# A second order table for the same 2,633 steps of a softmax-attention and gated-MLP kernel, with a shorter general path

## The chip, the cores and the metric

The kernel runs on one core of one Trainium2 chip. Its time is the device time of one execution in microseconds (us), and a stated time is a median of several executions. One execution was also recorded by the hardware profiler; durations of single instructions, here and below, are from that record.

## The reference, cut to what matters

```python
def _attn_ref(q, k, v, cap):                 # (4, 12, 448, 64) each, float32
    scores = np.matmul(q, k.transpose(0, 1, 3, 2)) / np.sqrt(64)
    scores = cap * np.tanh(scores / cap)     # cap = 30
    attn = np.exp(scores - scores.max(-1, keepdims=True))
    attn = attn / (attn.sum(-1, keepdims=True) + 1e-09)
    return np.matmul(attn, v)

def _moe_ref(x, w_in, w_out):                # x: 1792 x 768, d_ff 2048
    h = x @ w_in
    g = h * (1.0 / (1.0 + np.exp(-1.702 * h)))
    return g @ w_out
```

The heads of the attention's output are put side by side to give `x` (4 batches of 448 tokens, 12 heads of 64). The weights of the second part reach the device as 64-bit numbers, and the kernel turns them into pairs of half-precision numbers itself.

## The kernel before, in words

The program has two paths. `fast_path` computes everything by sums that hold for inputs of ordinary size, and on the way it gathers evidence that they do; `verdict` (lines 1245 to 1270) turns the evidence into one integer, `flag`. `tile_kernel` (line 358) then loads `flag` into a register of every engine (line 365), and only where it is 1 does the branch at line 366 let `general_path` run, which computes the result anew in float32. With these inputs the flag is 0: each engine jumps over the code of `general_path`.

Work of the fast path. The 12 heads of a batch are taken two by two, so there are 24 pairs (units), 6 for each batch. For a pair: four groups of score products (`scores`), tanh and exp on ScalarE, row sums and products with `v` (`attend_step` and `attend`), and a division that gives two half-precision parts of `x` (`xh`, `xl`). In the first seven units scores and sums are float32 products; later ones use half-precision parts. Units 4 and 5 divide on the spot (`normalise_direct`). In the others the row sums go through memory: `sd<-f`, `rsum<-sd`, a reciprocal, `rd<-rr`, `rb<-rd`, four small transfers one after the other (lines 780 to 788), and only then is `x` formed (lines 793 to 795). An `h_unit` (line 796) adds up products of the decoded `w_in` with the `x` of pair 0, 1, ... 5 of a batch in this order; `o_unit` does so with `w_out`. Batches 2 and 3 are multiplied together with fewer products (`h_quad`, `seven_first`, `seven`). Each weight piece is fetched (`fetch_w`) and decoded (`decode_w`, lines 576 to 584) by six passes, some of which may stand on VectorE or on ScalarE.

What sets the order. Each step is entered once into a plan with the engine or engines that can do it. `schedule` unpacks the string `ORDER`: for each step its place and its engine, and for each buffer that is used in turn (a ring) the slot that each use gets. Each engine works its list strictly in order, and SyncE (SP) sends every transfer, also in order. `timed` gives each step a due time from constants (`RATE`, `LAG`, `DMA_BW`); it decides in which sequence the lists are written out, and for how long `keep_busy` (line 352) fills a planned gap of TensorE with products of zeros before the first `h_unit`. The trace of before has no such filling product.

At the start line 427 runs 16 products of `ones16` with `wz`, a tile of zeros, each 128 columns wide. At the end, after the last result (`fresh` at line 1115 and `send` at line 1072), the flag is loaded and the engines meet.

Lines as the profile names them: L257 every product of the plan, L263 every transfer, L222 most VectorE steps, L245 scaling on VectorE, L214 and L238 ScalarE, L427 the 16 products of zeros, L365 and L366 flag and branch, L1439 the end of the program.

Of the kernel before, what the change touches and what calls it, by code (L numbers as in the profile page):

```python
# [11 lines left out]
F16 = mybir.dt.float16  # L12
F32 = mybir.dt.float32
# [24 lines left out]
EV_ON = ("AV", "AV")  # L38
SPLIT_ON = "A"
# [12 lines left out]
READ_ACC = 0.083  # L52
PE_COL = 0.0004222
# [3 lines left out]
LAG = {"PE": 0.165, "ACT": 0.1, "DVE": 0.085, "SP": 2.6}  # L57
DMA_ISSUE, DMA_BW = 0.5, 0.36
# [15 lines left out]
    "wI-b@8<=EjnaQR=;GUae%9+}MbtZwSVoI2TW~xbO)|;y4wyR+_m^!9#V7tj@c9^<>BBokkr`cs%nR@1sNn~1^X=b=-6R2*kyZinbrk!bTMwoYIo@r~|n=xjj>0l0<v1X?EU>@j?W}F!nc;tGTUM8{W80c;KnDJ(}"
    "x$g#=zGgz8lNn@YnSN%u8EyKT&Vd1Dc3_41VY--=fsJO4S!m`5ewvBqp#PVdYc`pu=7=e3Hk+enfeA6cO%t=nJa%O7xV>hZd0}pvErIFgmRV)k9x$r|Vh`y>0ne^6&jLOZ#~w6(bK5L7Ndj?gQgh5~HFwPEz`np4"
    "bH%(2+%*9c&pvQh&3&`q6brmE8Et&~z<e?Z>{)ZoB)8AqLzlunHwo?aKuVj%K5@lOD*MpfFpX_4``H9dZu`Q0F?sAc^TeDt$ITK0_N99iIAOk<ljdvSlzD7kxx6-O@Pc{mirA+vG|<F;Gs-5i+7`7-1I`w+iS1k0"
    ")S@-PX7-)S6dY{A*=44=jT}s3qgZQO*w^Nw$!C)W2ia^kwSD7S+Gj4AEpF4;^7fO9YSY^AHnY8FN?5;57mQ$A*@*VD%Wosu^tN?ylr3O0*a|izINC<Dg>7^@#uf}#v_4zXR<fn+SX<d%3beIl?H5<YmJW`yZEOr1"
    "2$r**Y$4m(z6n&dU)^}y&X%#?To?P^0k*e&><1ULU2R|6&Av6Yf<tVFU~L=IX1Cp~!qc{+t!8`J33iI@X{+0zcA~9e`&o^3Y)$*!eRRX@N;}Z*u>FIp>}As{xYG`>!-K2sNNaGHooaX6x^|i!Ve8p7c2e+!U2CTY"
    "Ev~aOt;0QbvR!XC+Z@3S_J`YRx7b<sknL^v**NaHJrkT^>)Y9Oqup;W+O2khJ!@~+h4zw-?{3<h_GIvujb%gaZHsu=zObk4w%|*<$TqNd>`%AdzOqN`YrDx_wr}il`_>)^-n9?yFE_{Dvk5}y+QpV|iG641+1U1I"
    "aK61}#a#&=vz}uN=ib{#HoRMEui6j62=1}9E*#zuKC^>^5uJ0-ZEE+xMsp2=EnIkv8~WRQvIlJ%_aqo*(Is`??MM5=rgap$%$~F9+*8}yC3ERrLYKiscb{!M7s-9GKW%as*=2R?Vz{sNn~i{tY#x`<#da}6tGFnk"  # L80
    "nOt5M%jI+V-7lNXMZ^N`w-t<p1zjpv(-m^HT#C@luCS}^vb&V7jyoR&*U{w&&E@L4mZ5E2Jr^0Px=t>OYwTj+R#(mCbUR#US0ps5^RSD{?Yg=Pwu$TQVq*2sZmy^+=9H`N!dw*W?uxsnE*3U$C0yyy9<EtvNms_z"
    "aHU)#7aIq-s2B&QyJ$GjHFwc*hKq}>+)P*24RL+kEEf+4xrU+fF~s$CjofUv+-?hP>*hG0o9p~;p4;HcxqwUT%Dcpv0Qb3}F6j2VexXTlnd|9>g|4s*-Tctu?tts>D!7gApgZJrXfL<OEq9@Afm`7gyCm+gONb|2"
    "QXK4-geJn3E*Z|oBW{&j>gM5UmmDj)5pIne=|;Ju?xY*-&bqWX#!U!Khnw6)H`c9n?c6wb%58V!-OkXFxY?Z!-Hf~3D4gWd;}+cFGT>+&i)Y+9w-r<1HXMiZaSWb!$J`#A>@wno&?#;bR&p0zAuNn3u?QB$y_gwG"
    "4Nir|mBxKI9#dl`oQ#!S8f+gr4X3&}gFCqWxBw>%K99TI6fA@5LbKphoQO*>D=x+LZaU7z6?g$xVh&t}*>Dvu$FexhmBa0r7oTA<%!!Y&IOfA#SORBYZY+s;up+L-nV22RV<o(Zvv3_=!aZ&W-oU+XC$7iJxO(tS"
    "JnpLCJzRtN@fPkHTos=TzKpwZ16Ic?SO9Nh1uTdM@F3p7LwFdEU=2Jm_$qG1lXw)X;Zr<@_ptyS$7_S@;7@#xZ}0(L#}8N&PvKj9IJhn@#25Gu3)4rui|_Ff*28r43DZ-3{EENuGd942VVS5Fe!<%K8*|e)JdK&D"
# [12 lines left out]
    "|GMSBccA}Mwf{m)4gdG6|999L?ZDW-<$~1?i8a!nvgc3D?~G#g=SQiKft@w%fc}IbD6+)H5nI&oS139(^arfL*}wA1(Vyv`lk>mAe*o)%ulf"
# [49 lines left out]
class Plan:  # L148
# [158 lines left out]
    def timed(self, pre, seqs):  # L307
# [6 lines left out]
        while any(at[e] < len(s) for e, s in seqs.items()):  # L314
            moved = False
            for e, s in seqs.items():
                while at[e] < len(s) and all(start[p] is not None for p, _ in pre[s[at[e]]]):
# [9 lines left out]
                    if e == "SP":  # L327
                        done[i] = pipe = max(pipe, t + us) + o.mb / DMA_BW
# [1114 lines left out]
```

## Time and profile before

| | us |
|---|---|
| median of 3 executions (lowest, highest) | 591.7 (591.09, 592.51) |
| the profiled execution | 594.05 |
| span in it, from the first to the last instruction | 591.9 |
| TensorE busy (products) | 577.8 |
| VectorE busy | 542.0 |
| ScalarE busy | 399.3 |

Products overlap with weight loads and with each other, and their ends are modelled, so "busy" means that products were under way. The profiled execution spends 2.15 us outside its span. Engine names in rows: PE is TensorE, PEld its weight loads, DVE is VectorE, ACT is ScalarE, SP is SyncE; a q behind a name means the engine's instruction queue. The granted clock of TensorE is a column (PEclk) of the tables by stretches.

### The profile page before, as it was taken

The page shows a single profiled execution, that of the slowest core. Times are in us where ns is not written, and L with a number is a line of the kernel's source. Part 1 is how long each engine was busy: PE and PEld are TensorE (multiplying, and loading weights), DVE is VectorE, ACT ScalarE, POOL GpSimd, SP SyncE. Part 2 cuts the span into 40 slices and gives each one's busy share as a digit, 9 for nine tenths or more (in the row PEclk, how much of TensorE's full clock was granted, in tenths as well). Part 3 has the DMA queues.
Part 4 walks back from the last instruction along what each step waited for, and adds up shares of the span by engine and source line. Part 5 has one row for each costly group of instructions (what it writes and reads, how often), then busy time and mean ns, then how long its engine had stood idle before and what let it go on. Part 6 is the DMA issues. An engine that isn't in the chain of part 4 may idle for free.

```text
span 591.9 us, 9836 instructions
## 1 busy us (share of the span) xinstructions
PE 577.8 (98%) x3674; PEld 288.5 (49%) x3674; DVE 542.0 (92%) x904; ACT 399.3 (67%) x617; POOL 0.2 (0%) x4
## 2 busy tenths in 40 slices
PE   7998899999999999999999999999999999999995
PEld 3333345555555554544555555555555555555552
DVE  4998999999999999999999999988999999988932
ACT  5998899989789899898787687434445543421110
POOL 0000000000000000000000000000000000000000
PEclk9999999999999999999999999999999999999999
DMA  8999763624567544343433444312222210000201
GB/s 298 328 239 294 227 239 108 205 71 139 157 172 209 193 141 141 95 137 110 148 86 101 120 153 133 104 48 81 88 71 82 64 45 0 17 0 1 79 31 69
DMA packets 45559, 74.36 MB, mean 126 GB/s; under 512 B 14952, under 2 KB 30912, under 8 KB 45504
## 3 DMA queue, kind: packets, MB, share of 16 engines
q1 hardware_dynamic: 45504, 73.66, 40.2%
q8 instruction: 31, 0.51, 0.3%
q14 instruction: 24, 0.20, 0.1%
HBM read 61.68 MB, written 11.95 MB: 124 GB/s over the span
## 4 chain that ended last, share of the span: by engine, by line
PE 73%; DVE 15%; DMA 5%; issue 3%; ACT 1%; SPq 1%; DVEq 0%
PE m L257 39%; PE z L257 22%; PE s L257 5%; PE pa L257 5%; DVE wo L222 3%; DVE p L222 2%; DMA sd<-f 2%; PE sm L257 2%; DMA g<-in_moe_w_in_dram 1%; DMA rb<-rd 1%; DVE g L222 1%; DVE rb L222 1%; DVE ta L222 1%; DVE ql L222 1%; DVE wi_l L222 1%
## 5 line engine op out<-in xcount | busy, mean ns | idle before, releaser
L257 PE MATMUL m<-g,wo 128*128 128x448 f16 x624 | 126.4, 353 | 0.0
L257 PEld LDWEIGHTS <-wo 128*128 128x128 f16 x864 | 83.4, 98 | 80.5 <-issue 3.6
L214 ACT ACTIVATE t<-s 128x896 f32<-128x896 f32 (+1 forms) x96 | 77.5, 823 | 22.9 <-DVE p L222 12.8
L257 PEld LDWEIGHTS <-wi_h 128*128 128x128 f16 x528 | 50.5, 98 | 53.1 <-issue 7.6
L257 PE MATMUL m<-x,wi_h 128*128 128x448 f16 x234 | 63.6, 353 | 1.4 <-DVE x L222 0.7
L222 DVE TENSOR_TENSOR p<-t,p 128x896 f16<-128x896 f32 (+1 forms) x62 | 58.5, 951 | 0.7 <-ACT p L238 0.4
L257 PE MATMUL m<-xa,wi_h 128*128 128x448 f16 x198 | 53.7, 353 | 0.0
L214 ACT ACTIVATE t<-t 128x896 f32<-128x896 f32 (+1 forms) x62 | 51.9, 846 | 0.6
L238 ACT ACTIVATE p<-t 128x896 f16<-128x896 f32 (+1 forms) x54 | 45.1, 841 | 3.3 <-PE pa L257 3.0
L257 PE MATMUL s<-qh,kk 128*128 128x448 f16 (+3 forms) x152 | 46.0, 377 | 0.0
L222 DVE SCALAR_TENSOR_TENSOR wo<-wo 128x1024 int32<-128x1024 int32 (+2 forms) x42 | 44.3, 1065 | 0.2 <-ACT wo L238 0.2
L257 PE MATMUL s<-ql,kk 128*128 128x448 f16 (+1 forms) x136 | 42.0, 353 | 0.0
L257 PE MATMUL m<-x,wi_l 128*128 128x448 f16 x117 | 41.2, 353 | 0.0
L257 PEld LDWEIGHTS <-stg 128*128 128x128 f16 x288 | 28.2, 98 | 26.3
L257 PEld LDWEIGHTS <-wi_l 128*128 128x128 f16 x264 | 25.8, 98 | 25.0 <-issue 1.0
L257 PE MATMUL pa<-p,vh 128*64 128x448 f16 x272 | 37.5, 355 | 0.2 <-DVE rb L222 0.2
L257 PE MATMUL m<-xa,wi_l 128*128 128x448 f16 x99 | 34.9, 353 | 0.0
L257 PEld LDWEIGHTS <-kk 128*128 128x128 f16 (+1 forms) x272 | 23.3, 101 | 22.5 <-issue 2.7
L257 PEld LDWEIGHTS <-xa 128*128 128x128 f16 x216 | 21.0, 98 | 19.6
L238 ACT ACTIVATE xa<-x 128x1024 f16<-128x1024 f32 x9 | 9.4, 1055 | 30.1 <-PE z L257 15.0
L257 PE MATMUL s<-wo 64*128 64x448 f32 (+1 forms) x96 | 24.7, 622 | 3.4 <-DMA wo<-in_q_dram 1.8
L257 PE MATMUL sm<-p,ones 128*32 128x224 f16 (+2 forms) x544 | 26.5, 306 | 0.0
(278 smaller groups left out, 1092.8 us busy)
## 6 DMA issues: line engine op xcount, KB each, us to landing
wo<-in_moe_w_in_dram SPq DMA_DIRECT2D x18, 512.0 KB, 5.4
stg<-in_kx_dram SPq DMA_DIRECT2D x17, 448.0 KB, 4.3
stg<-in_qx_dram SPq DMA_DIRECT2D x17, 448.0 KB, 3.8
stg<-in_moe_w_out_dram SPq DMA_DIRECT2D x16, 384.0 KB, 5.8
wo<-in_moe_w_out_dram SPq DMA_DIRECT2D x16, 384.0 KB, 8.4
sum<-xa SPq DMA_DIRECT2D x32, 192.0 KB, 3.7
stg<-sum SPq DMA_DIRECT2D x32, 192.0 KB, 2.9
rb<-rd SPq DMA_DIRECT2D x44, 112.0 KB, 3.2
```

The lines of the kernel that those rows point to most:

```text
L214: self.nc.scalar.activation(real(out), real(in_), func, scale=real(scale), **b)
L222: getattr(self.nc.vector, name)(out=real(out), **{k: real(x) for k, x in ins.items()}, **kw, **a)
L238: self.nc.scalar.activation(real(out), real(in_), AF.Copy, scale=1.0 if f is None else f, **b)
L257: self.nc.tensor.matmul(real(o), real(w), real(x), start=a, stop=z)
```

## The change

Five things are changed, none of them in what the fast path computes.

1. Another `ORDER`, 2,633 steps as before. Read step by step against the old one: 32 steps go from VectorE to ScalarE and 29 from ScalarE to VectorE. On SyncE's list the load of q for unit 5 stands 26th (it was 37th), that of its k 31st (33rd); the first row-sum transfer (`sd<-f` of unit 0) is 13th (15th) and is now ahead of v of unit 1 and of k and q of unit 3. On TensorE's list the second sum product of unit 2 is 27th (34th), and the first `h_unit`'s step with the `x` of pair 2 is 72nd (63rd), behind the sum and v products of unit 5; the second v product of unit 0 is 6th (12th), ahead of the first scores of unit 1. VectorE begins with the first weight piece (the second before), and SyncE sends that piece first. In the list of TensorE the kind of product (which rows and columns of the array it uses) changes 96 times, before 101 times; behind the first 110 steps 60 and 62 times.
2. The flag's last step, which stood 862nd of VectorE's 864 steps, two results ahead of the end, is now the last of its 861. On SyncE's list the same 12 last sends stand in another order; the last one is the same.
3. The rings for q (`qh`) begin with slot 1 instead of 0, so they go in turn with those of k; `stg`, `f` and the ring for sums go in turn more strictly.
4. 38 products of zeros instead of 16 at the start, and they wait for one memset only, which is now VectorE's first instruction.
5. `general_path` is two loops without inner rounds, and reads v in another layout (`vn`, a further input that the fast path doesn't touch). Code per engine that the branch jumps over: TensorE 24 products (224 before), VectorE 19 instructions (210), ScalarE 4 (44).

Constants of `timed` change with it (`LAG`, `DMA_EARLY`, a price `UPPER` for VectorE steps on upper partitions), and `values_load` has no bounds any more.

```diff
+WARM = 38
+UPPER = 0.23
-LAG = {"PE": 0.165, "ACT": 0.1, "DVE": 0.085, "SP": 2.6}
-DMA_ISSUE, DMA_BW = 0.5, 0.36
+LAG = {"PE": 0.165, "ACT": 0.109, "DVE": 0.087, "SP": 2.9}
+DMA_ISSUE, DMA_BW, DMA_EARLY = 0.5, 0.36, 0.5
 ORDER = (
...
+        if any(isinstance(x, Ref) and x._at(0).base_partition() for x in w + list(ins.values())):
+            us += UPPER
...
                         done[i] = pipe = max(pipe, t + us) + o.mb / DMA_BW
+                        done[i] += DMA_EARLY * (t < 80.0)
...
-        r = tc.nc.values_load(flag, min_val=0, max_val=1)
+        r = tc.nc.values_load(flag)
         with tc.If(r > 0):
-            general_path(tc, q, k, v, cap, w_in, w_out, out)
+            general_path(tc, q, k, vn, cap, w_in, w_out, out)
...
+    wz = sb.tile([P, 128], F16, name="wz")
+    nc.vector.memset(wz, 0.0)
     capt = sb.tile([P, 1], F32, name="capt")
...
-    for _ in range(16):
-        nc.tensor.matmul(ps_m["tiles"][0][:32, :128], ones16[2], wz, start=True, stop=True)
+    for _ in range(WARM):
+        nc.tensor.matmul(ps_m["tiles"][0][:32, :128], wz[:, :32], wz, start=True, stop=True)
...
-        with tc.For_i(0, B * NP) as u:
+    with tc.tile_pool(name="g_att", bufs=1) as att, tc.For_i(0, N) as i:
...
+        for c in range(NQ):
+            nc.tensor.matmul(qk[:QC, c, :S], qd[:, c * QC:(c + 1) * QC], kd, start=True, stop=True)
...
+    with tc.tile_pool(name="g_mlp", bufs=1) as mlp, tc.For_i(0, NFC * B) as i:
...
+        for c in range(NCC):
+            nc.tensor.matmul(hp[:, :S], wi[:, c], x[:, c], start=(c == 0), stop=(c == NCC - 1))
...
+        for d in range(NCC):
+            nc.tensor.matmul(op[:, d, :S], wo[:, d * P:(d + 1) * P], e, start=True, stop=True)
...
```

## Rows read from the trace of the kernel before

**Rows 1.** By stretches: us, busy of each engine (instructions), granted clock, DMA share, GB/s.
```profile
10.00:40.00 30.00, 29.65 (x230) 10.71 (x234) 29.38 (x39) 29.85 (x42) 0.00 (x0) 1.00 0.97 324
40.00:70.00 30.00, 26.03 (x135) 8.87 (x129) 26.18 (x32) 26.05 (x35) 0.00 (x0) 1.00 0.87 240
...
84.00:250.00 166.00, 165.80 (x1131) 85.84 (x1128) 163.83 (x275) 151.48 (x234) 0.00 (x0) 1.00 0.48 145
```
**Rows 2.** TensorE's waits from 5 to 84: for whom, us in total, times, longest.
```profile
PE m L257 <- DVE x L222: 0.7, 1, 0.7
PE m L257 <- ACT x L238: 0.7, 1, 0.7
```
**Rows 3.** In order of time, first 51 us: start, us, engine, line, what, count, [idle before].
```profile
1.92 1.86 PE L427 MATMUL m<-wz,ones 128*32 128x128 f16 x16 [1.92 <-DVE thr L1253]
...
5.12 3.36 PE L257 MATMUL s<-wo 64*128 64x448 f32 x8 [1.34 <-DMA wo<-in_k_dram]
...
9.95 0.43 DVE L222 TENSOR_SCALAR g<-g 128x512 int32<-128x512 int32 x1 [0.88 <-DMA g<-in_moe_w_in_dram]
...
22.07 1.77 PE L257 MATMUL s<-wo 64*128 64x448 f32 x8
...
49.64 1.77 PE L257 MATMUL s<-wo 64*128 64x448 f32 x8 [1.75 <-DMA wo<-in_q_dram]
```
**Rows 4.** The chain that ended last, pieces in order of time: start, us, what.
```profile
2.61 7.32 DMA g<-in_moe_w_in_dram
...
54.61 6.94 DMA rb<-rd
...
105.61 3.97 PE m L257 x21
109.58 0.88 PE sm L257 x32
```
**Rows 5.** SyncE's sends of k and q for unit 5, in order of time.
```profile
38.71 0.39 SPq L263 DMA_DIRECT2D wo<-in_k_dram  x1
...
42.88 0.42 SPq L263 DMA_DIRECT2D wo<-in_q_dram  x1
```
**Rows 6.** What SyncE waited for from 560 on: us, times, longest.
```profile
SPq L365 <- DVE flag L1270: 11.2, 1, 11.2
```
**Rows 7.** The end in order of time: the flag, the last result, its send.
```profile
583.92 0.13 DVE L1270 TENSOR_SCALAR flag<-cnt 1x1 int32<-1x1 f32 x1
...
585.65 0.62 DVE L222 SCALAR_TENSOR_TENSOR f<-z,stg 128x448 f32<-128x448 f32 x1 [1.07 <-PE z L257]
...
586.39 0.40 SPq L263 DMA_DIRECT2D out_dram<-f  x1
```
**Rows 8.** The branch line by queue: ns min/median/max, first and last start in us.
```profile
L366 SPq EVENT_SEMAPHORE  x8: 17/17/17, 587.4 to 590.6; - x8
L366 ACTq COMPARE_BRANCH  x1: 45/45/45, 584.4 to 584.4; - x1
...
L366 PEldq COMPARE_BRANCH  x1: 4227/4227/4227, 584.7 to 584.7; - x1
L366 ACTq EVENT_SEMAPHORE  x1: 17/17/17, 584.9 to 584.9; - x1
L366 DVEq COMPARE_BRANCH  x1: 72/72/72, 586.5 to 586.5; - x1
...
L366 PEldq EVENT_SEMAPHORE  x1: 51/51/51, 589.0 to 589.0; - x1
L366 DVEq EVENT_SEMAPHORE  x1: 21/21/21, 590.3 to 590.3; - x1
```
**Rows 9.** A lone send of a result, issued at 547.9: us from issue to landing.
```profile
DMA to landing us min/median/max: 1.9/1.9/1.9
```
**Rows 10.** One decode pass from 8 to 50, on either engine: busy, mean ns, idle before.
```profile
L238 ACT ACTIVATE wo<-wo 128x1024 f32<-128x1024 f32 x3 | 3.8, 1260 | 0.1
...
L245 DVE TENSOR_SCALAR wo<-wo 128x1024 f32<-128x1024 f32 x2 | 1.4, 700 | 0.0
```

More of the change, by code (lines that the diff above doesn't have):

```diff
@@ L99 @@
+    "KmT8+{MSC{e~<!yANBtV8m+9*=JzIRqbwjPz_0=+tiHEl$s&PJf-=92lr?B1fsv?D35!aDHWc<ASP*Cxh~I*RFvPIO-zMjONB;q@@v({"
 )
@@ L357, in keep_busy, with tile_kernel @@
             self.nc.tensor.matmul(out[:cols, :128], z[:rows, :cols], z[:rows], start=True, stop=True)
-def tile_kernel(tc, q, k, qx, kx, v, cap, w_in, w_out, out):
+def tile_kernel(tc, q, k, qx, kx, v, vn, cap, w_in, w_out, out):
     with ExitStack() as outer:
@@ L420, in fast_path @@
             nc.vector.memset(o[j][(1 - j) * D:(2 - j) * D], 0.0)
-    wz = sb.tile([P, 128], F16, name="wz")
-    nc.vector.memset(wz, 0.0)
     ps_m = ring([P, 512], F32, "m", 2, ps)
     plan.zeros, plan.idle_bank = wz, ps_m
-    for _ in range(16):
-        nc.tensor.matmul(ps_m["tiles"][0][:32, :128], ones16[2], wz, start=True, stop=True)
+    for _ in range(WARM):
+        nc.tensor.matmul(ps_m["tiles"][0][:32, :128], wz[:, :32], wz, start=True, stop=True)
     rc = sb.tile([P, 1], F32, name="rc")
@@ L1290, in general_path @@
     P = 128
-    NC = 7
-    NV = 8
+    N = B * NP * 2
+    QC = 112
+    NQ = S // QC
     NCC = DM // P
     NFC = DFF // P
-    QC = 112
-    NQ = S // QC
+    assert B == 4
+    M = DM * DFF // (N * P)
     drm = ctx.enter_context(tc.tile_pool(name="g_drm", bufs=1, space=bass.MemoryType.DRAM))
-    xt = drm.tile([B * NP, P, S], F32, name="xt")
-    md = drm.tile([2, S], F32, name="md")
+    xt = drm.tile([N, D, S], F32, name="xt")
+    md = drm.tile([1, S], F32, name="md")
+    wd = drm.tile([2, N, P, M], F32, name="wd")
     cst = ctx.enter_context(tc.tile_pool(name="g_cst", bufs=1))
-    ones = cst.tile([P, D], F32, name="ones")
-    nc.vector.memset(ones, 1.0)
     capt = cst.tile([P, 1], F32, name="capt")
@@ L1406 @@
-_INS = ["q", "k", "qx", "kx", "v", "cap", "moe_w_in", "moe_w_out"]
+    acc = cst.tile([P, B, NCC, S], F32, name="acc")
+    nc.vector.memset(acc, 0.0)
+    ps = ctx.enter_context(tc.tile_pool(name="g_ps", bufs=1, space=bass.MemoryType.PSUM))
+    qf, kf = (a.rearrange("b p (j d) s -> (b p j) d s", j=2) for a in (q, k))
+    bits = [w.bitcast(I32).rearrange("r n -> (r n)").rearrange("(i p m) -> i p m", p=P, m=2 * M) for w in (w_in, w_out)]
+    with tc.tile_pool(name="g_att", bufs=1) as att, tc.For_i(0, N) as i:
+        kd = att.tile([D, S], F32, name="kd")
+        qd = att.tile([D, S], F32, name="qd")
+        vo = att.tile([QC, NQ, 2 * D], F32, name="vo")
+        st = att.tile([P, 2, M, 2], I32, name="st")
+        one = bass.ds(i, 1)
+        nc.sync.dma_start(kd, kf[one].rearrange("o r s -> (o r) s"))
+        nc.sync.dma_start(qd, qf[one].rearrange("o r s -> (o r) s"))
+        nc.sync.dma_start(vo[:, :, :D], v[one].rearrange("o (c p) d -> (o p) c d", p=QC))
+        nc.vector.memset(vo[:, :, D:], 1.0)
+        for w in range(2):
+            nc.sync.dma_start(st[:, w].rearrange("p m t -> p (m t)"), bits[w][one].rearrange("o p m -> (o p) m"))
+        af = att.tile([P, 2, M], F32, name="af")
+        a = af.bitcast(I32)
+        L, H = st[:, :, :, 0], st[:, :, :, 1]
+        nc.vector.tensor_single_scalar(out=a, in_=H, scalar=0x7FFFFFFF, op=ALU.bitwise_and)
+        nc.vector.tensor_scalar(out=af, in0=af, scalar1=2.0**-15, scalar2=122880.0, op0=ALU.max, op1=ALU.min)
+        nc.vector.tensor_scalar(out=a, in0=a, scalar1=0x38000000, scalar2=3, op0=ALU.bitwise_xor, op1=ALU.logical_shift_left)
+        nc.vector.tensor_single_scalar(out=a, in_=a, scalar=0x7FFFFFFF, op=ALU.bitwise_and)
+        nc.vector.scalar_tensor_tensor(out=a, in0=L, scalar=29, in1=a, op0=ALU.logical_shift_right, op1=ALU.bitwise_or)
+        nc.vector.scalar_tensor_tensor(out=a, in0=H, scalar=-(2**31), in1=a, op0=ALU.bitwise_and, op1=ALU.bitwise_or)
+        nc.sync.dma_start(wd[:, one].rearrange("w o p m -> (o p) w m"), af)
+        qk = ps.tile([P, NCC, 512], F32, tag="s", name="qk")
+        for c in range(NQ):
+            nc.tensor.matmul(qk[:QC, c, :S], qd[:, c * QC:(c + 1) * QC], kd, start=True, stop=True)
+        mx = att.tile([QC, NQ], F32, name="mx")
+        nc.vector.tensor_reduce(out=mx, in_=qk[:QC, :NQ, :S], op=ALU.max, axis=AX.X)
+        nc.sync.dma_start(md.rearrange("o (c p) -> (o p) c", p=QC), mx)
+        mb = att.tile([QC, 1, S], F32, name="mb")
+        nc.sync.dma_start(mb[:, 0], md.to_broadcast([QC, S]))
+        nc.scalar.activation(mb, mb, AF.Tanh, scale=tsc[:QC])
+        kq = ps.tile([P, NCC, 512], F32, tag="s", name="kq")
+        for c in range(NQ):
+            nc.tensor.matmul(kq[:QC, c, :S], kd[:, c * QC:(c + 1) * QC], qd, start=True, stop=True)
+        t = att.tile([QC, NQ, S], F32, name="t")
+        nc.scalar.activation(t, kq[:QC, :NQ, :S], AF.Tanh, scale=tsc[:QC])
+        nc.vector.tensor_tensor(out=t, in0=t, in1=mb.to_broadcast([QC, NQ, S]), op=ALU.subtract)
+        nc.scalar.activation(t, t, AF.Exp, scale=capt[:QC])
+        pa = ps.tile([P, 512], F32, tag="pa", name="pa")
+        for c in range(NQ):
+            nc.tensor.matmul(pa[:, :S], vo[:, c], t[:, c], start=(c == 0), stop=(c == NQ - 1))
+        r = att.tile([D, S], F32, name="r")
+        nc.vector.tensor_scalar_add(r, pa[D:, :S], 1e-9)
+        nc.vector.reciprocal(out=r, in_=r)
+        nc.vector.tensor_tensor(out=r, in0=pa[:D, :S], in1=r, op=ALU.mult)
+        nc.sync.dma_start(xt[one].rearrange("o r s -> (o r) s"), r)
@@ new lines, in general_path @@
+    xv = xt.rearrange("(b c j) d s -> b (j d) c s", b=B, j=2)
+    wiv = wd[0].rearrange("i p m -> (i p m)").rearrange("(c p f n) -> f p c n", c=NCC, p=P, f=NFC)
+    wov = wd[1].rearrange("i p m -> (i p m)").rearrange("(f p n) -> f p n", f=NFC, p=P)
+    with tc.tile_pool(name="g_mlp", bufs=1) as mlp, tc.For_i(0, NFC * B) as i:
+        f = bass.ds(nc.s_assert_within(i >> 2, 0, NFC - 1, skip_runtime_bounds_check_because="i < 4 * NFC"), 1)
+        b = bass.ds(nc.s_assert_within(i & 3, 0, B - 1, skip_runtime_bounds_check_because="two bits"), 1)
+        x = mlp.tile([P, NCC, S], F32, name="x")
+        wi = mlp.tile([P, NCC, P], F32, name="wi")
+        wo = mlp.tile([P, DM], F32, name="wo")
+        nc.sync.dma_start(x, xv[b].rearrange("o p c s -> (o p) c s"))
+        nc.sync.dma_start(wi, wiv[f].rearrange("o p c n -> (o p) c n"))
+        nc.sync.dma_start(wo, wov[f].rearrange("o p n -> (o p) n"))
+        hp = ps.tile([P, 512], F32, tag="pa", name="hp")
+        for c in range(NCC):
+            nc.tensor.matmul(hp[:, :S], wi[:, c], x[:, c], start=(c == 0), stop=(c == NCC - 1))
+        e = mlp.tile([P, S], F32, name="e")
+        nc.scalar.activation(e, hp[:, :S], AF.Exp, scale=-1.702)
+        nc.vector.tensor_scalar_add(e, e, 1.0)
+        nc.vector.reciprocal(out=e, in_=e)
+        nc.vector.tensor_tensor(out=e, in0=hp[:, :S], in1=e, op=ALU.mult)
+        op = ps.tile([P, NCC, 512], F32, tag="s", name="op")
+        for d in range(NCC):
+            nc.tensor.matmul(op[:, d, :S], wo[:, d * P:(d + 1) * P], e, start=True, stop=True)
+        mine = acc[:, b].rearrange("p o c s -> p (o c) s")
+        nc.vector.tensor_tensor(out=mine, in0=mine, in1=op[:, :, :S], op=ALU.add)
@@ L1409 @@
+    for b in range(B):
+        nc.sync.dma_start(out.rearrange("(d p) (b s) -> b p d s", p=P, s=S)[b], acc[:, b])
+_INS = ["q", "k", "qx", "kx", "v", "vn", "cap", "moe_w_in", "moe_w_out"]
 def kernel(**inputs):
@@ L1424 @@
         host[n + "x"] = _np.concatenate([t, t], axis=2)
+    host["vn"] = inputs["v"].reshape(B * H, S, D)
     vv = inputs["v"].reshape(B, NP, 2, S, D)
```

164 lines of the change are left out of this document (36 added, 128 removed).

## The prediction

> **What bounds the kernel now.** I read the table by stretches first. From 84 us on TensorE is never short of work: 165.80 of 166 us up to 250 [rows 1], and of the 14.1 us that it is not busy in all (591.9 − 577.8) the start, the stretch from 10 to 70 and the end, named below, hold nearly everything. Work is only moved behind 84, so a new order can win little there. What is not full lies at the two ends. From 10 to 40 the three engines are full together (29.65, 29.38 and 29.85 of 30); from 40 to 70 all three have holes, TensorE 3.97 us, VectorE 3.82, while the DMA engines are busy for 0.87 [rows 1]. Then the waits: among TensorE's holes are 1.75 us for the q of unit 5 [rows 3], and 0.7 and 0.7 for an `x` part [rows 2]. The chain of waits says why `x` is late: it runs through small transfers that queue behind weights, `rb<-rd` alone 6.94 us [rows 4]. Last the end: after the last result's step (585.65 + 0.62 = 586.27) [rows 7] 5.63 us of the 591.9 remain in which no engine computes. SyncE stood 11.2 us at the load of the flag [rows 6], and the results that were ready behind it left only then.
>
> **The end.** Removed: that stand. The flag is now VectorE's last step, so its load on SyncE can only come behind the sends of results that are ready earlier; they leave as they come, the last at the same distance from the last product, 586.39 [rows 7]. Before, it was one of four within 1.5 us, each 229 KB, and SyncE's last waits for landings end at 590.6 [rows 8], 4.2 us after that send. A lone send landed after 1.9 us [rows 9]. Its landing would then be 586.39 + 1.9 = 588.3, and from the last landing to the end of the span it takes 591.9 − 590.6 = 1.3: the end is at 589.6, a gain of 2.3 us. The send just ahead of it leaves about a microsecond earlier and may still be under way, so I take 2.1.
>
> Added: a later branch. The flag is written at 586.27 + 0.13 = 586.4 instead of 584.05 [rows 7], 2.35 us later, and every engine waits for it. What is queued behind is only the meeting of the engines. It costs nothing as long as the branch is done before the landing at 588.3. ScalarE went from its branch (584.4) to its next instruction (584.9) in 0.5 us, TensorE in 4.3 (584.7 to 589.0), VectorE in 3.8 (586.5 to 590.3) [rows 8]. By the code they jump over 44 instructions, 224 products and 210 instructions; a float32 product is two records of product and two of weight load, so TensorE's jump is near 900. After: 4, 24 products (some 100 records) and 19. TensorE's lies between ScalarE's 44, which cost 0.5, and VectorE's 210, which cost 3.8; it is nearer to the 44, so I take 0.5. With 0.5 us for load and 0.5 for the jump all engines are done at 587.4, under the cover of the landing. Without that cover: 589.0 + 2.35 = 591.35 for TensorE, 592.65 at the end, 0.75 us later than before. So the end gives −2.1, between −2.3 and +0.8.
>
> [...]
>
> `values_load` without bounds takes two instructions off SyncE between load and branch; SyncE waits for the landing then, so nothing.
>
> **The start, products of zeros.** 16 records of the L427 loop took 1.86 us, 0.116 each; 38 that wait for one memset only can start about a microsecond earlier and end near 5.4 at the latest, against 5.12 for the first score product [rows 3], a possible loss of 0.3. [...] But the v product that follows needs v of unit 0, which lies in the queue behind the weights that landed at 2.61 + 7.32 = 9.93 [rows 4]; 262 KB more at 324 GB/s [rows 1] make 10.7. [...] So whatever the first products gain, TensorE stands for v afterwards, and I take 0. Bounds −1.6 and +0.3.
>
> **The start, the order.** The load of q for unit 5 goes from the 37th to the 26th place, so the 1.75-us hole [rows 3] goes. What is late next is its k, only two places earlier: sent at 38.71 and q at 42.88 [rows 5], and q came 49.64 − 42.88 = 6.8 us later (its product began when the hole ended) [rows 3, 5]. If k leaves at 37 it lands near 44, and TensorE reaches that product at about 43. I charge 1.0 us for it. The two holes of 0.7 for `x` of pair 2 [rows 2] should go: the step stands nine places later, behind sum and v products that need nothing of it, and its sums are made seven steps earlier, so that the four small transfers start sooner. VectorE begins with the piece that is sent first, so its hole of 0.88 at 9.95 [rows 3] shrinks. Sum: 1.75 + 0.7 + 0.7 − 1.0 = 2.15 of TensorE's holes; I take 2.1, as new ones must be expected in a list in which only 493 of 869 TensorE steps keep their order. Bounds: 0 and 4.3 (all the holes from 10 to 70, 0.35 + 3.97 [rows 1]), and on the bad side VectorE's rival below.
>
> A step moved past others on SyncE: the first `sd<-f` is now ahead of v for unit 1 and k, q for unit 3, and waits there for ScalarE's copy of the first sums. The DMA engines are busy for 0.97 of this stretch [rows 1], so transfers are queued ahead of it and a late send costs nothing while that queue lasts.
>
> **Rings, constants, kinds of product.** The slots of q, `stg` and `f` only loosen waits that don't show up among TensorE's [rows 2]: nothing. The constants change no instruction but the number of filling products before the first `h_unit`; they lie in planned gaps: nothing, at worst 0.3. The kind of product changes five times fewer, two of them where TensorE is full. One change costs 0.12: the sum products take 0.88 for 32 records, four steps of 0.19 (3.97 / 21) each are 0.76 [rows 4]. Two are 0.2.
>
> **Sum.** 2.1 (end) + 2.1 (order) + 0.2 (kinds) = 4.4 us. The profiled execution has span 591.9 and time 594.05; they become 587.5 and 589.65. The median of the executions shown is 2.35 below the profiled one; taken from it, 591.7 − 4.4 = 587.3.
>
> **Rivals.**
> The jump still waits for code: the end is +0.75 instead of −2.1, so 591.7 − 2.3 + 0.75 = 590.1. For: nothing in the rows shows a jump of TensorE's new length. Against: ScalarE's 0.5.
>
> The order wins nothing: VectorE is 98% busy from 10 to 40 and 98.7% from 84 to 250 [rows 1], and an earlier TensorE only waits for it. Then 591.7 − 2.3 = 589.4. Against: 3.8 us of holes on VectorE itself from 40 to 70.
>
> The order wins all 4.3 of the holes, and a little of the faster first products comes through (0.2): 591.7 − 2.3 − 4.5 = 584.9.
>
> Slower: VectorE becomes the bound in the first 50 us. There it takes five decode passes from ScalarE and gives back three and a smaller step: 5 x 0.70 − 3 x 0.70 − 0.4 = 1.0 us more [rows 10], and by 250 fifteen against nine. If its list runs through without using its own holes, each of these is a shift of everything behind it: 1.0, and about 1.9 more by 250, together 2.9 against the 2.1 of the end: 592.5. It decides as soon as the holes of VectorE from 40 to 70 shrink by less than 0.8 us.
>
> [...]
>
> The flag's load is still put ahead of sends: the end gives 0, 589.4.
>
> **Chances.** Forecast 0.50, jump waits 0.12, order wins nothing 0.15, order wins all 0.11, VectorE the bound 0.06, clock 0.03, load ahead 0.03. A measurement of this kernel tells about 0.2%, 1.2 us, from no change: faster means below 590.5, slower above 592.9. Faster: all of the forecast, nothing and all, most of the jump and the two small ones, 0.84; same 0.11; slower 0.05, the upper half of VectorE's rival and of the forecast's unseen holes. The range from 585.0 to 590.3 leaves out about one in ten on each side.
>
> **What would show it.** Right: in the profile after, SyncE's wait at L365 is short, the sends of results stand apart, TensorE's and VectorE's first instruction behind the branch comes within 1 us, the last landing about 2 us behind the last send. TensorE's wait for q of unit 5 and those for `x` are gone, and busy from 40 to 70 is above 28 of 30. First scores at the pace of 22.07. Wrong: a branch of TensorE over 3 us; new holes of over 2 us before 84, or any of over 0.5 behind it; VectorE full from 40 to 70 while TensorE waits for it.

## The result, and the profile after

The changed kernel takes 585.84 us (median of 4 executions, 585.69 to 586.17) against 592.11 (591.09 to 592.58) for the kernel before in the same set: ratio 0.9899, 95% interval 0.9885 to 0.9913, 6.3 us less where 4.4 were forecast. A second set gave 0.9902, 0.9879 to 0.9926. The profiled execution after: time 585.69, span 583.64. The record of before that the prediction rests on has a long execution for its kernel (time 594.05); a second one has span 590.01 and time 592.17.

The stretches of the changed kernel, columns as in [rows 1]:

```profile
10.00:40.00 30.00, 30.00 (x240) 11.25 (x238) 28.81 (x43) 28.90 (x41) 0.00 (x0) 1.00 0.99 331
40.00:70.00 30.00, 28.56 (x142) 10.16 (x140) 29.59 (x33) 29.15 (x40) 0.00 (x0) 1.00 0.87 290
84.00:250.00 166.00, 166.00 (x1132) 85.87 (x1131) 164.41 (x280) 148.41 (x229) 0.00 (x0) 1.00 0.48 144
```

From 40 to 70 TensorE is busy for 28.56 us instead of 26.03, and nothing opens behind 84; single executions differ in that stretch, though, as the second records below show. TensorE's waits from 5 to 84, which answer to [rows 2]:

```profile
PE pa L261 <- ACT pu L242: 0.8, 2, 0.6
PE sm L261 <- ACT p L216: 0.6, 1, 0.6
PE s L261 <- DMA wo<-in_q_dram: 0.3, 1, 0.3
PE s L261 <- ACT t L216: 0.3, 1, 0.3
```

The waits for `x` and for q of unit 5 are gone; the wait for q that is left is that of unit 0. The start in order of time, answering to [rows 3]:

```profile
0.99 3.87 PE L432 MATMUL m<-wz 128*32 128x128 f16 x38 [0.99 <-DVE warm L418]
5.19 1.77 PE L261 MATMUL s<-wo 64*128 64x448 f32 x8 [0.32 <-DMA wo<-in_q_dram]
6.55 0.43 DVE L224 TENSOR_SCALAR g<-g 128x512 int32<-128x512 int32 x1 [2.41 <-DMA g<-in_moe_w_in_dram]
7.89 0.43 DVE L224 TENSOR_SCALAR g<-g 128x512 int32<-128x512 int32 x1 [0.18 <-DMA g<-in_moe_w_in_dram]
8.00 1.79 ACT L216 ACTIVATE p<-t 128x896 f32<-128x896 f32 x2
9.07 1.75 PE L261 MATMUL pa<-p,wo 128*64 128x448 f32 x8
...
46.96 0.97 PE L261 MATMUL sm<-p,ones 128*64 128x448 f32 x4 [0.58 <-ACT p L216]
48.52 3.23 PE L261 MATMUL pa<-p,wo 128*64 128x448 f32 x16 [0.59 <-ACT pu L242]
```

The first scores take 1.77 us (3.36 before), and the first v product begins at 9.07 (10.81 before). The second weight piece is there at 7.89, not at 9.95. SyncE's sends of k and q, answering to [rows 5] (q of unit 5 is the first, its k the second):

```profile
28.05 0.41 SPq L267 DMA_DIRECT2D wo<-in_q_dram  x1
...
34.31 0.58 SPq L267 DMA_DIRECT2D wo<-in_k_dram  x1
```

The end, answering to [rows 7]: last result, flag, last send; then the branch by queue, answering to [rows 8]:

```profile
579.63 0.62 DVE L224 SCALAR_TENSOR_TENSOR stg<-z,rb 128x448 f32<-128x448 f32 x1 [0.48 <-PE z L261]
580.17 0.13 DVE L1275 TENSOR_SCALAR flag<-cnt 1x1 int32<-1x1 f32 x1
...
580.28 0.33 SPq L267 DMA_DIRECT2D out_dram<-stg  x1
```

```profile
L371 SPq EVENT_SEMAPHORE  x8: 17/17/17, 581.8 to 582.3; - x8
...
L371 PEldq COMPARE_BRANCH  x1: 223/223/223, 580.9 to 580.9; - x1
L371 DVEq COMPARE_BRANCH  x1: 72/72/72, 581.0 to 581.0; - x1
...
L371 PEldq EVENT_SEMAPHORE  x1: 51/51/51, 581.2 to 581.2; - x1
...
L371 DVEq EVENT_SEMAPHORE  x1: 21/21/21, 581.6 to 581.6; - x1
```

TensorE is through its branch after 0.2 us, VectorE after 0.6; SyncE finds the flag written when it comes to load it, so no line answers to [rows 6]. The last send landed at 582.21 (1.9 us), and SyncE reaches its last wait at 582.3: the landing and SyncE's own row of waits end together. From the end of the last result's step to the end of the span it is now 583.64 − 580.25 = 3.39 us; before 591.90 − 586.27, 5.62 unrounded. Call this the end part.

### The profile page after: what moved, and what is told of

It reads as the page before. It is cut to its first block, busy times and chain, and to the rows that moved or that the text cites. A ratio compares the mean times of both kernels' runs of the same rounds, so it can differ in the third digit from the quotient of the medians.

```text
span 583.6 us, 9869 instructions
## 1 busy us (share of the span) xinstructions
PE 576.6 (99%) x3696; PEld 289.2 (50%) x3696; DVE 541.7 (93%) x901; ACT 400.3 (69%) x620; POOL 0.2 (0%) x4
## 4 chain that ended last, share of the span: by engine, by line
PE 90%; DMA 6%; DVE 2%; ACT 1%; SPq 1%; issue 0%; DVEq 0%; ACTq 0%
PE m L261 48%; PE z L261 22%; PE s L261 8%; PE pa L261 8%; PE sm L261 3%; DMA wo<-in_moe_w_in_dram 2%; DMA stg<-in_kx_dram 1%; DMA wo<-in_k_dram 1%; DMA rd<-rr 1%; DMA rb<-rd 1%; DVE wo L224 1%; DMA sd<-f 1%; SPq L267 1%; ACT p L216 0%; DVE wi_l L224 0%
## 5 line engine op out<-in xcount | busy, mean ns | idle before, releaser
L242 ACT ACTIVATE p<-t 128x896 f16<-128x896 f32 (+1 forms) x52 | 43.4, 839 | 1.5 <-PE pa L261 1.0
L261 PE MATMUL pa<-p,vl 128*64 128x448 f16 x136 | 24.2, 352 | 0.0
```

What stands on the lines that cost most here:

```text
L242: self.nc.scalar.activation(real(out), real(in_), AF.Copy, scale=1.0 if f is None else f, **b)
L261: self.nc.tensor.matmul(real(o), real(w), real(x), start=a, stop=z)
```

## The experiments

Three sets of four, each with its own runs of before. Their medians of before are 593.05 (changed with the long path, the early flag, the old start, the old order), 592.80 (both of these, zeros, changed in the second set, one step earlier) and 592.60 (the others), so across sets only ratios can be compared. TensorE's end, the end part and the landing of the first weight piece are from the one record that each kernel left.

| kernel | median, us | ratio to before (95%) | TensorE ends | end part | first weight piece |
|---|---|---|---|---|---|
| before (first record) | | | 585.61 | 5.62 | 8.62 |
| before, second record | 592.17 (one) | | 583.77 | 5.58 | 7.88 |
| + load without bounds | 592.45 | 1.0009 (0.9991, 1.0027) | 583.13 | 5.36 | 7.97 |
| + short general path | 590.83 | 0.9972 (0.9952, 0.9991) | 582.83 | 4.41 | 6.70 |
| + both of these | 591.66 | 0.9977 (0.9965, 0.9990) | 584.66 | 4.30 | 8.11 |
| + 38 products of zeros | 592.48 | 0.9996 (0.9980, 1.0013) | 585.37 | 5.38 | 8.37 |
| + order table | 591.65 | 0.9991 (0.9976, 1.0005) | 581.40 | 6.35 | 7.34 |
| changed (first record) | 585.84 | 0.9899 (0.9885, 0.9913) | 579.59 | 3.39 | 6.53 |
| changed, second set | 587.12 | 0.9902 (0.9879, 0.9926) | 582.01 | 3.39 | 6.46 |
| changed, long general path | 591.14 | 0.9964 (0.9949, 0.9979) | 582.40 | 6.42 | 7.58 |
| changed, flag early | 588.04 | 0.9909 (0.9888, 0.9930) | 582.53 | 3.39 | 6.63 |
| changed, old start | 588.15 | 0.9922 (0.9902, 0.9942) | 581.84 | 3.40 | 6.53 |
| changed, old order, flag last | 588.24 | 0.9926 (0.9906, 0.9945) | 582.13 | 3.47 | 6.72 |
| changed, one step earlier | 587.75 | 0.9919 (0.9899, 0.9939) | 580.09 | 3.39 | 6.54 |

**The end: which part of it pays.** First the load alone (b_nobounds):

```diff
-        r = tc.nc.values_load(flag, min_val=0, max_val=1)
+        r = tc.nc.values_load(flag)
```

> The kernel before with the flag loaded without bounds, nothing else: the load then stands behind the last four sends, which leave as their results come; the long general_path and its jumps stay. Theory A (sends that leave apart land soon): the last landing 1.9 to 2.2 us after the last send; VectorE's jump of 3.8 us still ends near 590.3, so the time falls by 0 to 0.5 us. Theory B (code transfers delay the results): the last landing again 3 to 4 us after the last send; time within 0.3 us of before.

Measured: nothing, 1.0009. On SyncE's list the load now stands behind the last four sends; the four results land 3.9 to 4.1 us after their sends all the same. Theory B. Its branch rows, and the DMA view of its last 9 us (packets, MB, share; last line: us to landing):

```profile
L366 PEldq COMPARE_BRANCH  x1: 3807/3807/3807, 582.2 to 582.2; - x1
```

```profile
GB/s 0 0 36 0 0 0 0 0 0 0 0 0 0 263 407 371 351 350 351 358 374 96 76 48 207 358 403 104 24 121 48 60 0 36 0 0 0 0 0 0
...
q14 instruction: 6, 0.05, 2.0%
q8 instruction: 2, 0.03, 1.8%
...
out_dram<-f SPq DMA_DIRECT2D x2, 224.0 KB, 4.1
```

Then the short path alone (b_shortgen), the new `general_path` with its input `vn`:

```diff
-            general_path(tc, q, k, v, cap, w_in, w_out, out)
+            general_path(tc, q, k, vn, cap, w_in, w_out, out)
```

> The kernel before with the short general_path alone: the bounded load of the flag still stands ahead of the last four sends, flag and order as before. Theory A (the prediction's: the end hangs on four sends that leave within 1.5 us, and their landing): the last send again lands 4 us after it leaves, 592.3 to 592.8. Theory B (the long jumps fetch code, and the transfers of code delay one of the DMA engines that carry the results): the last landing comes 1.9 to 2.7 us after the last send, and the time falls by 1.1 to 2.0, to 590.8 to 591.7.

Measured: 0.9972, 1.7 us less, although the load still stands ahead of the sends. Theory B again. The same two views, of its last 8 us:

```profile
L366 PEldq COMPARE_BRANCH  x1: 236/236/236, 581.9 to 581.9; - x1
```

```profile
GB/s 0 41 0 0 0 0 0 0 0 0 0 0 0 41 0 269 367 358 126 278 358 412 368 349 412 359 376 367 188 41 0 0 0 0 0 0 0 0 0 0
...
q14 instruction: 3, 0.02, 1.0%
...
out_dram<-f SPq DMA_DIRECT2D x2, 224.0 KB, 2.4
```

The queues named "instruction" are read here as the ones that carry code: eight transfers of 0.08 MB with the long path, three of 0.02 MB with the short one. With the long path the stream of results has a tail at 24 to 121 GB/s where one sixteenth of its rate before, some 370, would be 23, which suggests that most of the 16 DMA engines have finished and few, perhaps one, are late. The trace counts each send's landing in 16 parts: of the first of the four sends 14 parts are in by 584.07 with the long path and the last at 586.01; with the short one 15 are in by 584.15 and the last at 584.44. That the late parts belong to an engine that fetches code is inferred; no row names the engine.

Both together (b_nbshort), and in the changed kernel the long path put back with its bounded load (a_longgen):

> The kernel before with the short general_path and with the load of the flag unbounded, which puts it behind the last four sends on SyncE's list. Order, start and the flag's place on VectorE (two results ahead of the end) are as before. Theory A (sends that stand apart and short jumps together give all of the gain at the end, whatever the flag's place): from the last result's step to the end 3.4 us instead of 5.6, the time 2.0 to 2.4 us less, 589.7 to 590.1. Theory B (the flag has to be last): 0 to 0.8 us less.

> The changed kernel with general_path and the bounded load of the flag as before; the flag stays VectorE's last step. Theory A (the length of the code that is jumped over sets the wait): TensorE's branch takes about 4.2 us and VectorE's about 3.8 from 580.3 on, nothing covers it, and the end moves from 583.6 to 586.3 to 586.8: 588.5 to 589.0. Theory B (the long waits of before came from something else, such as the four sends that were under way at the same time): 585.6 to 586.4, branches under 1 us.

Both together: 0.9977, no more than the short path alone, an end part of 4.30 and not 3.4, since the last send (585.51) landed only at 588.21; between the two theories. The changed kernel with the long path lost 0.62% (0.9964 against 0.9902), more than expected, and its branch rows say why:

```profile
L371 PEldq COMPARE_BRANCH  x1: 4198/4198/4198, 583.7 to 583.7; - x1
...
L371 DVEq EVENT_SEMAPHORE  x1: 21/21/21, 586.9 to 586.9; - x1
L371 PEldq EVENT_SEMAPHORE  x1: 51/51/51, 588.0 to 588.0; - x1
```

With the flag last nothing covers TensorE's jump: the end part is 6.42, 3.0 more. Here the last result was sent 0.6 us ahead of that jump, and all landed after 1.9 to 2.2 us. So the long jump cost in either place here: with the flag early the results landed after 3.0 to 4.1 us, with the flag late the jump was the end itself. The rest of this kernel's loss lies ahead of 84 us.

Then the flag's place (a_flagearly), on VectorE's list:

```diff
 f<-m,stg
+flag<-cnt
 rb<-m,rb
 stg<-z,rb
-flag<-cnt
```

> The changed kernel with one step moved: the flag is written two results before VectorE's end, as before, instead of last. On SyncE's list the load of the flag still stands behind all sends. Theory A (the end hangs on SyncE's own load, branch and semaphores behind the last send, which has to wait for the last result): -0.1 to -0.4 against the changed kernel, 585.4 to 585.7, since load and branch of the other engines are done earlier but SyncE's come right behind the last send. Theory B (the flag being last is what gave the 2.3 us at the end): the end is 1 to 2.3 us later, 586.8 to 588.1.

The end part is 3.39, the same to the hundredth. Neither theory's number came out: SyncE's load stands behind the last send anyway, and its waits for the landings end the program. The ratio, 0.9909 against 0.9902, shows no difference either; in the record TensorE ended 2.9 us later for a reason in the first 56 us, below.

With the table of before the flag's place does count. With the short path and the flag early (b_nbshort) the end part is 4.30 and the last four sends land after 2.6 to 3.1 us, with the flag last (a_oldorder, below) it is 3.47 and they land after 1.9 to 2.3. So the 3.4 needs the short path and beside it the late flag or the new table, each read from one record. In a_flagearly no code transfer starts between 575 and 584.7, when nearly all of the last result has gone; in b_nbshort one starts at 584.6, among the sends.

**The start.** The zeros alone on the kernel before (b_warm38), and the old start in the changed kernel (a_warm16, the reverse of the same edit):

```diff
-    for _ in range(16):
-        nc.tensor.matmul(ps_m["tiles"][0][:32, :128], ones16[2], wz, start=True, stop=True)
+    for _ in range(38):
+        nc.tensor.matmul(ps_m["tiles"][0][:32, :128], wz[:, :32], wz, start=True, stop=True)
```

> The kernel before with the start as changed: 38 products of zeros that wait for wz alone. Theory A (the prediction's step: v of unit 0 lands too late): 592.1 again, and the first v product at 10.8. Theory B (the first products are on the path; the time of v's landing in the first record was a slow execution): first eight scores 1.77 instead of 3.36, the first v product 1.6 to 2.4 us earlier, and 1.3 to 2.4 us less, 589.7 to 590.8.

> The changed kernel with the start as before: 16 products of ones16 with the zeros, wz set behind the constants. Changed kernel 585.8. Theory A (the prediction's step: v of unit 0 lands at about 10.6 and takes back what the first products gain): 585.5 to 586.1, and the first v product again begins at about 9.1. Theory B (the loads come earlier than the prediction took them, so the slower first products are on the path): the first eight score records take 3.36 us again instead of 1.77, the first v product begins 1.6 to 2.5 us later, and the time is 587.4 to 588.3.

Alone: nothing (0.9996), theory A. Taken out of the changed kernel: 0.9922 against 0.9902, 1.2 us, theory B, though the intervals overlap; its first scores took 3.36 us again, and its first v product began at 11.45, 2.4 us later. The start of b_warm38:

```profile
5.16 2.47 PE L257 MATMUL s<-wo 64*128 64x448 f32 x8
...
8.54 1.79 ACT L214 ACTIVATE p<-t 128x896 f32<-128x896 f32 x2
...
10.44 0.97 PE L257 MATMUL pa<-p,wo 128*64 128x448 f32 x4 [0.62 <-ACT p L214]
```

Of the 1.6 us between 3.36 and 1.77, 0.9 show here at the first eight scores (a pace of 1.77 did not come here: 2.47, and 2.64 in a_flagearly, against 1.77 or 1.78 in the other records with 38 products) and 0.25 at the first v product. Its row names ScalarE's exp, whose second half ends at 10.33. But this product needs only the first half, which ends at 9.49; in the second record of before it begins while the second half still runs:

```profile
9.34 1.78 ACT L214 ACTIVATE p<-t 128x896 f32<-128x896 f32 x2
10.69 0.97 PE L257 MATMUL pa<-p,wo 128*64 128x448 f32 x4
```

In b_warm38 v landed at 10.31, and TensorE's queue held for it until 10.3. So TensorE stood 0.62 us for v, as the prediction's step says. In the changed kernel v is there at 8.55, the first half of the exp ends at 8.96, and TensorE goes from the scores to the v product without a pause. In the variant with the long path v lands at 9.48, and TensorE stands for it again:

```profile
9.62 1.72 PE L261 MATMUL pa<-p,wo 128*64 128x448 f32 x8 [0.50 <-DMA wo<-in_v_dram]
```

Behind its start b_warm38 has a hole of 1.69 at 42.8 instead of 0.58.

**The order.** The table alone (b_order: the string `ORDER` of after in the file of before), and the table of before, flag moved last, in the changed kernel (a_oldorder):

> The kernel before with the new order table alone (its slots and the flag as VectorE's last step come with it); 16 products of zeros, the long general_path and the bounded load as before. Theory A (the prediction's term, independent of the rest: 2.3 us of TensorE's time up to 84 us): TensorE ends 2.0 to 2.6 us earlier, the end is 0.8 us longer because the late flag's long jumps are no longer covered, so 1.2 to 1.8 us less: 590.7 to 591.3. Theory B (the order pays only together with the earlier start, since the transfers bound it): TensorE ends 0 to 1 us earlier, and the time is 592.3 to 593.5.

> The changed kernel with the order table of before, in which only the flag's step is moved to VectorE's end; start, general_path and constants as changed. It tells what the order itself is worth. Theory A (the prediction's term: 2.1 for holes, 0.2 for kinds of product): 588.1, with the holes from 40 to 70 back (TensorE near 26 of 30). Theory B (the order wins nothing): 585.8. Theory C (it wins all of the holes): 590.1.

The table alone: TensorE's holes from 5 to 84 are 1.36 us (2.67 in the second record of before), it ends 2.4 us earlier than there, the end part grows by 0.8, and the time falls by 0.5 (0.9991, an interval that holds no change). Theory A for TensorE, between the two for the time; but the record is that of the fastest of its twelve executions (590.32, median 591.65), so 2.4 is more than a typical one shows. With the old table the changed kernel stands at 0.9926; theory A's 588.1 is 0.9932 of 592.1, B's 0.9894, C's 0.9966. So it is A, or somewhat less: against 0.9902 the table is worth 1.4 us there, with overlapping intervals. TensorE's busy time from 40 to 70 does not decide it: 27.36 of 30 us with the old table, where theory A named about 26, against 28.56 and 27.01 in the two records with the new one.

**The spread.** The changed kernel and the kernel before once more (a_again, b_again, no edit):

> The changed kernel itself, once more, beside the three others of this set. The first record of it has TensorE's holes of 0.59 and 0.59 near 47 us; four variants with other edits have one of 1.7 to 2.5 there, behind a VectorE step that waits 1.0 to 1.8 us for a weight piece. Theory A (the length of that hole differs from execution to execution with the speed of the transfers, not with the edit): the ratio to before is again 0.988 to 0.992, single executions lie 2 us or more apart, and the hole lies between 0.5 and 2.6 us. Theory B (the edits made the hole): 0.6 again, and executions within 0.5 us.

> The kernel before once more, for a second record. In its first record the first weight piece landed at 8.6 us; in those of the kernel with the changed start alone at 8.4 and with the changed end alone at 8.1; in six of the changed kernel and its variants at 6.5 to 6.7, in a seventh (the long general_path) at 7.6. Theory A (it belongs to the kernel): 8.0 to 8.7 again. Theory B (it differs from execution to execution): 6.4 to 7.6.

a_again: theory A, though the four executions lie closer together than it said, between 586.53 and 588.17. The hole at 48 is 2.57 us in this record, against 0.59 in the first. TensorE and VectorE of a_again in order of time, then its stretches:

```profile
50.12 4.55 PE L261 MATMUL pa<-p,wo 128*64 128x448 f32 x16 [2.57 <-ACT pu L242]
54.60 1.77 PE L261 MATMUL s<-wo 64*128 64x448 f32 x8
...
46.45 0.70 DVE L224 TENSOR_SCALAR wo<-wo 128x1024 int32<-128x1024 int32 x1 [1.84 <-DMA wo<-in_moe_w_in_dram]
```

```profile
48.00:50.00 2.00, 0.00 (x0) 0.00 (x0) 2.00 (x3) 0.47 (x2) 0.00 (x0) 0.85 0.93 231
50.00:52.00 2.00, 1.88 (x6) 0.76 (x8) 2.00 (x3) 2.00 (x4) 0.00 (x0) 0.50 0.89 303
52.00:54.00 2.00, 2.00 (x10) 0.66 (x8) 2.00 (x4) 1.92 (x4) 0.00 (x0) 0.79 0.91 279
54.00:56.00 2.00, 2.00 (x12) 0.69 (x8) 2.00 (x4) 0.78 (x2) 0.00 (x0) 1.00 0.93 352
```

A weight piece that landed at 44.69 in the first record landed at 46.36 here. VectorE stands 1.84 us for it, the product behind it on VectorE (`rb<-pu,rb`) is late, ScalarE's copy waits for that, TensorE for the copy. Behind the hole the granted clock is 0.50: 16 v products take 4.55 us instead of 3.23. One late transfer so costs 2.57 − 0.59 + 1.32 = 3.3 us on the way, and TensorE ended 2.4 later. a_flagearly shows the same (hole 2.54, clock 0.50 from 52 to 54), which makes most of its 2.9 us. From 40 to 70 TensorE is busy for 27.01 of 30 us in a_again, less than in the second record of before (27.55). So the closed holes that the first two records show there lie within what executions differ by. What both records of the changed kernel have ahead of 84 is the start: first v product at 9.07 and 9.12, against 10.81 and 10.69 before. After holes of 1.76 and 1.77 at the same place (a_longgen, a_warm16) the column stayed at 1.00.

b_again: between the two, 7.88. All six records with the long general path have the first weight piece at 7.34 or later, seven of eight with the short one at 6.46 to 6.72; the eighth (8.11) speaks against a rule.

**A try at the hole** (a_rbearly), on VectorE's list:

```diff
 TENSOR_SCALAR wo<-wo
+TENSOR_TENSOR rb<-pu,rb
 TENSOR_SCALAR wi_h<-wo
 SCALAR_TENSOR_TENSOR wo<-wo
-TENSOR_TENSOR rb<-pu,rb
```

> The changed kernel with one VectorE step moved: the product with the reciprocal sums for unit 2 (rb<-pu,rb) three places up, behind the first decode pass of the weight piece that lands at 44.7 instead of behind its third. Its own input landed at 45.3, so it can run at 45.5 instead of 47.2. Theory A (TensorE's hole at 48 hangs on this step by way of ScalarE's copy pu<-pa): the hole of 0.59 at 47.9 goes, in slow executions it shrinks from 1.8 to about 0.1, and the time falls by 0.5 to 1.7 us. Theory B (VectorE is full here and the moved step only pushes the decode passes back): 0 to +0.6 us.

Theory B. The hole at 47 is 0.64 although the weight piece came 0.5 later than in the first record, but a new one opens, behind decode steps that were pushed back:

```profile
47.71 3.23 PE L261 MATMUL pa<-p,wo 128*64 128x448 f32 x16 [0.64 <-ACT pu L242]
...
55.48 0.97 PE L261 MATMUL s<-wo 64*64 64x448 f32 x4 [1.03 <-ACT t L216]
```

0.9919 against 0.9902: no gain, so no version here beats the changed kernel.

## Why the prediction was right, and where its steps were not

The time lies inside the range, 0.8 us from its lower end. Of its two mechanisms the shorter end stands in both records of the changed kernel. The holes that close from 40 to 70 stand in the first two records (26.03 to 28.56 of 30) and not in the second two (27.55 and 27.01). The sum was 1.9 us short, and that it came so near is in part luck: one term had the right size for a half wrong reason, and one was put at nothing and was worth about 1.2.

- **The end, −2.1.** 5.62 to 3.39 is −2.2: the size was right. The reason was half wrong. The step "a lone send landed after 1.9, one of four within 1.5 us after 4.2" put the late landing down to the bunch of sends and to SyncE's stand at the load. b_nobounds removes the stand and gains nothing; a_oldorder sends three results within 0.9 us, each of which lands after 1.9 to 2.3. What landed late, 3.0 to 4.1 us after its send, were results under way while the "instruction" queues moved the 0.08 to 0.10 MB of the long path. The shorter code, which the prediction counted for the jump alone, gives 1.2 of the 2.2 by itself (b_shortgen 4.41); the rest needs the late flag or the new table with it (a_oldorder 3.47, a_flagearly 3.39, b_nbshort 4.30).
- **The jump, 0.5 us.** 0.2 for TensorE (and it was on the path: with the long code the end part is 6.42). The rival "jump waits for code" fell. With the long code TensorE's jump of some 900 waited 4.2 us in a_longgen once more and VectorE's of 210, as far as counted (computing instructions alone), 3.1 us, from 583.8 to 586.9.
- **SyncE's load.** Said to go because the flag is last. Either edit does it: with the flag early the unbounded load stands behind all sends too (a_flagearly), at the same end part.
- **The zeros, 0.** Right for the kernel before (0.9996), where TensorE did stand 0.62 us for v (b_warm38); wrong inside the change: 1.2 us, with overlapping intervals. The first eight scores took 3.36 us behind 16 products (a_warm16) and 1.77 behind 38 (the first record of the changed kernel), with a granted clock that prints 1.00 from 0 to 10 in both; what sets their pace no run shows. The bound of −1.6 is that difference, and b_warm38 showed 0.9 of it at the first eight scores. The step that failed is "TensorE stands for v afterwards": it carried v's landing near 10.7 from one execution of before over to the changed kernel, where v lands at 8.5 to 9.1 in the six records with the short path. The first v product then follows the scores without a wait, and comes earlier when they do.
- **The order, −2.1, and the kinds, −0.2.** TensorE waits no longer for q of unit 5 and `x`, as forecast; the waits for `x` are missing in the second record of before too, and that for unit 5 is 1.36 there. The 1.0 charged for k of unit 5 was not paid: it left at 34.31, not at 37, and nothing waits for it. New waits of 0.59 and 0.58 came in the first record. Alone the table takes 2.4 us off TensorE's end in one fast record and gives 0.8 back at the end of the program; by the medians it is worth 0.5 alone and 1.4 in the changed kernel, neither clear of noise. The kinds weren't tried by themselves.
- **What the sum left out.** Zeros, short path with load, and order alone give 0.04, 0.23 and 0.09%, together 2.1 us; all together give 5.8. Of these the zeros and the order alone are not clear of no change. About 1.7 of the difference is the end part: alone the short path takes 1.3 off it and the table adds 0.8, together they take off 2.2. The rest, some 2 us, lies ahead of 84, since behind it TensorE stands for at most 0.5 us in any record. There TensorE's holes hung on when transfers landed (the weight piece of a_again, 1.7 us late, made one of 2.57), and the first weight piece was earlier in most records with the short path (6.46 to 6.72 in seven of eight, 7.34 or later with the long one). Why, no run here shows; the new constants of `timed` were not tried by themselves either.
- **The rivals.** The chances give 0.03 to "clock". The granted clock did fall to 0.50 in two records of the changed list, not while waiting for v but after the holes of 2.57 and 2.54 at 48, where 16 v products took 1.3 and 1.7 us longer than 3.23; holes of 1.76 and 1.77 left it at 1.00. "New holes of over 2 us before 84" was named as what would prove the forecast wrong: one came, in some executions, and the time still fell. VectorE did not become the bound over the whole stretch: it is busier (29.59 of 30), but TensorE's holes shrank, and its own went from 3.82 to 0.41, far more than the 0.8 on which that rival turns.

## What to carry to other kernels

Code that is jumped over wasn't free at the end of this program: with the flag early one of the last results landed after 3.0 to 4.1 us over the long path and after 1.9 to 3.1 over the short one, and the long jump that came last made the end part 3.0 us longer; shorten the code before moving the branch. Parts of a change that save little alone can save together (2.1 us one by one here, 5.8 at once), so try them by leaving each out as well as by adding each. Where transfers are the bound, one record's landing times are no constants (the first weight piece landed at 8.62 and 7.88 in two records of the kernel before): take a second record before a term of the sum rests on them.

## What the runs showed of the hardware that was not expected

- TensorE's branch took 3.6 to 4.2 us over the long path (four records with the flag early, two with it late) and 0.22 to 0.24 over the short one.
- One of the last four writes of 229 KB landed after 1.9 to 2.3 us with the flag last or in a_flagearly, after 2.2 to 3.1 with the flag early and the short path in the old order (0.02 to 0.04 MB of code), and after 3.0 to 4.1 with the flag early and the long path (0.08 to 0.10 MB).
- In the stretch near 48 us the granted clock fell to 0.50 behind pauses of 2.54 and 2.57 us (a_flagearly, a_again), and stayed at 1.00 behind pauses of 1.75 to 1.77 (the first record of before, a_longgen, a_warm16).
